# Attention and a routed MoE on one core: rows scattered one tile per iteration, the last three tiles routed each alone

## The chip, the cores and the metric

One core of a Trainium2 chip. The metric is the device time of one execution in microseconds. TensorE is PE here, VectorE DVE, ScalarE ACT, GpSimd POOL, and SyncE SP; SP only issues transfers.

## The reference

Three layers, one after another, in float32. First a linear attention with decay, for 2 batches, 8 heads, 768 steps and 48 columns per head:

```python
for t in range(S):
    cur = einsum('bhd,bhe->bhde', u * k[t], v[t])
    y[t] = einsum('bhd,bhde->bhe', r[t], state + cur)
    state = w * state + einsum('bhd,bhe->bhde', k[t], v[t])
```

Its output, as 1536 tokens of 384 columns, goes through a mixture of 8 experts. Each token goes to the expert with the largest logit `x @ w_gate`; its place within the expert is the number of earlier tokens that chose the same one, and places from the capacity (384) on are dropped. Expert e computes `relu(x @ w1[e]) @ w2[e]`, and the result is multiplied by the token's softmax probability. The third layer is a gated one: `(silu(x @ w_gate) * (x @ w_val)) @ w_out`, with an inner width of 1536.

## The kernel before

The 1536 tokens are 12 tiles of 128. Attention runs as a software pipeline over `it` from -4 to 12, written out by hand (lines 358 to 411): every engine executes its instructions in the order in which this loop issues them. In iteration `it` the loop finishes tile `it` and prepares later ones:

- `outputs(it)`: PE sums the tile's result in `y` (lines 294, 300). `d_major(it)`: ACT copies it to `xT` (line 312; for the last three tiles DVE copies half, line 309).
- `logits(it - 1)`: DVE sums the router's logits (line 450), ACT copies the tile, token by row, to `xu` (line 452; four buffers).
- `state_update(it + 1)`: DVE adds `zt` (line 285), POOL multiplies it to the new state `Z` (line 286).
- `diag_dve(it + 3)`, `diag_act(it + 3)`: DVE reduces `ruk` to `c` (line 243), ACT makes the diagonal of `AT` from it (line 252).
- `diag_pool(it + 4)`: POOL computes `ruk` (lines 236, 237) and `kd` (line 239).
- `inner(it + 2)`: PE's products into `A` (line 259), DVE selects them into `AT` (line 266).
- `decay(it + 3)`: DVE makes `RK` (line 231).
- `token_major(it)`: PE turns `xT` into `xl` (line 443). `state_pe(it + 2)`: PE sums `U` (line 274).
- `prefetch(it - 3)`: SP loads a block `raw` of expert 0's weights (line 574).

Tiles are routed in batches, `BATCHES`. In iteration `it` the batch whose last tile is `it - 1` is routed: `route1` finds each token's expert (6 small DVE instructions and one of ACT, lines 463 to 470), `place_pe` counts earlier tokens on PE (line 486), `route2` computes probability and row (DVE, lines 493 to 514). Then, for every tile of the batch, ACT scales the rows `xu` by the probability (line 518) and POOL scatters them to their rows of `x_disp` in HBM by an indirect DMA (line 519). All scatters write `x_disp`, so each waits for the landing of the one before it, and a load from `x_disp` waits for the scatters before it; a scatter that follows a load waits for that load.

Expert 0 starts without waiting for the last three tiles' scatters. Its first 224 rows come from two sources: `xr0`, loaded from `x_disp` once tiles 0 to 8 are scattered (SP, line 593, issued in iteration 9 behind those scatters) and turned by PE (`first_rows`, line 350), and the last three tiles, each added by a product of `xu` with a one-hot matrix `hot` made in `route2` (line 508; `first_add`, line 342). These sums are copied out of PSUM as `x_plain` (line 608), and the expert's first products follow (line 742). The scaled rows of the last three tiles go to `xs`, since `xu` is still needed.

Expert 1's block `xr` is loaded by SP from `x_disp` behind all scatters (line 593), and PE turns it in the middle of expert 0's second half (line 711). Between the two loads of `xr` SP issues four blocks `raw`; behind the second one it issues expert 1's and later weights. `place_id` scatters token numbers to `ids` on POOL during expert 1 (line 795). After the experts follows the gated layer. `general` (line 1007) is a second path that these inputs do not take.

Of the kernel before, what the change touches and what calls it, by code (L numbers as in the profile page):

```python
# [15 lines left out]
AF = mybir.ActivationFunctionType  # L16
# [9 lines left out]
NT = B * NCH  # L26
# [25 lines left out]

NLAST = 3

BATCHES = [(0, 3), (3, 6), (6, 9), (9, 11), (11, 12)]
NBT = 3
FF_WEIGHTS = {"w_gate": [P, KD, 256], "w_val": [P, KD, 256], "w_out": [P, 2, DM]}

# [5 lines left out]
class Kernel:  # L64
# [44 lines left out]
    def attention(self, st):  # L109
        tc, nc, a = self.tc, self.nc, self.a  # L110
# [45 lines left out]
        def warm(n):  # L156
# [7 lines left out]
            out=tmpm, in_=ones, pattern=[[1, P]], compare_op=ALU.is_gt, fill=0.0, base=0, channel_multiplier=-1  # L164
# [16 lines left out]
        for part in (y[:, 0:3], y[:, 3:], U):  # L181
# [18 lines left out]
            out=neq, in0=sq[:, 0], scalar=1.0, in1=w_dm, op0=ALU.mult, op1=ALU.not_equal, accum_out=nbad  # L200
# [3 lines left out]
        for i in range(7):  # L204
            n = 1 << i
# [15 lines left out]

        RK, AT, cc, ruks = {}, {}, {}, {}
        xTs = self.xTs = {}
        self.xl, self.xu, self.batches = {}, {}, BATCHES
        self.row = cp.tile([P, NT], I32, name="row")

        def decay(i):
# [109 lines left out]
        def first_add(i, first, last):  # L337
            xu, _, hot = self.last[i]
            if first:
                px.extend(self.pa_tile() for _ in range(KD))  # L340
            for k in range(KD):
                nc.tensor.matmul(
                    px[k][:, 0:BLK], lhsT=xu[:, k * P:(k + 1) * P], rhs=hot, start=first, stop=last,
                    skip_group_check=True,
                )

        def first_rows(first):
            for k in range(KD):
                for t in range(2):
                    nc.tensor.matmul(  # L350
                        px[k][:, t * BP:(t + 1) * BP], lhsT=self.xr0[:, t, k * P:(k + 1) * P],
                        rhs=ident[0:BP, 0:BP], start=first, stop=first, skip_group_check=True,
                    )
# [4 lines left out]
        for it in range(-4, NT + 1):  # L358
            batch = ends.get(it - 1)
            if ok(it):  # L360
                outputs(it)
                d_major(it)
            if ok(it - 1):
                self.logits(it - 1)
            if it == NT:
                first_add(NT - 2, False, False)
                first_rows(False)
            if batch:
                self.route1(*batch)
            if has_state(it + 1):  # L370
                state_update(it + 1)
            if it == NT:
                self.route2(*batch)
                first_add(NT - 1, False, True)
            if it < 0 and ok(it + 3):
                decay(it + 3)
                load_T(it + 3 + NB)
            if ok(it + 3):
                diag_dve(it + 3)
                diag_act(it + 3)  # L380
            if ok(it + 4):
                diag_pool(it + 4)
                load_rk(it + 4 + NB)
            if ok(it + 2):
                inner(it + 2)
            if batch and it < NT:
                self.place_pe(*batch)
            if it >= 0 and ok(it + 3):
                decay(it + 3)
                load_T(it + 3 + NB)  # L390
            if batch and it < NT:
                self.route2(*batch)
            if it == -3:
                late_tables()
            if it in (-1, 2, 4):
                load_v({-1: 3, 2: 6, 4: 9}[it])
            if it in (-2, 0):
                first = (it + 2) // 2 * ST
                self.clear_rows(self.x_disp[first:first + BLK])
            if it == NT - 1:  # L400
                first_add(NT - 3, True, False)
            if ok(it):
                self.token_major(it)
            if has_state(it + 2):
                state_pe(it + 2)
            if it == NT - NLAST:
                self.x_load(0, self.xr0)
            if it >= 3:
                self.prefetch(it - 3)
            if it in WARMS:  # L410
                warm(WARMS[it])
# [3 lines left out]
            self.x_part_plain(self.x0, k)  # L415
        self.counts = cp.tile([P, E], F32, name="counts")
        self.count()

    def route_rooms(self):
        tp = self.tp  # L420
# [33 lines left out]
    def route1(self, lo, hi):  # L454

        nc, tp, n = self.nc, self.tp, hi - lo
        b3 = lambda x: x.unsqueeze(2).to_broadcast([P, n, E])
        over_tiles = lambda x: x.unsqueeze(1).to_broadcast([P, n, E])
        small = lambda name: tp.tile([P, NBT, E], F32, name=name, tag=name, bufs=1)[:, 0:n]
        lg, oh = self.lg[:, 0:n], self.oh[:, lo:hi]  # L460
        m = self.m = tp.tile([P, 6, NBT], F32, name="m", tag="m", bufs=2)[:, :, 0:n]
        dif, eqr, ex = small("dif"), small("eqr"), small("ex")
        nc.vector.tensor_reduce(m[:, 0], lg, AX.X, ALU.max)
        nc.vector.tensor_sub(dif, lg, b3(m[:, 0]))
        nc.scalar.activation(ex, dif, AF.Exp)
        nc.vector.scalar_tensor_tensor(
            out=eqr, in0=dif, scalar=0.0, in1=over_tiles(self.rev), op0=ALU.is_ge, op1=ALU.mult
        )
        nc.vector.tensor_reduce(m[:, 1], eqr, AX.X, ALU.max)
        nc.vector.tensor_tensor(oh, eqr, b3(m[:, 1]), ALU.is_equal)  # L470
        self.ex = ex
        if n == 1:
            self.place_pe(lo, hi)

    def place_pe(self, lo, hi):

# [13 lines left out]
    def route2(self, lo, hi):  # L490
        nc, tp, n = self.nc, self.tp, hi - lo
        m, pos = self.m, self.posall[:, lo:hi]
        nc.vector.tensor_reduce(m[:, 2], self.ex, AX.X, ALU.add)
        nc.vector.tensor_scalar(out=m[:, 2], in0=m[:, 2], scalar1=1e-9, scalar2=None, op0=ALU.add)
        nc.vector.reciprocal(m[:, 3], m[:, 2])
        nc.vector.tensor_scalar(
            out=m[:, 1], in0=m[:, 1], scalar1=-float(ST), scalar2=float(E * ST), op0=ALU.mult, op1=ALU.add
        )
        sc = tp.tile([P, NBT, E], F32, name="sc", tag="sc", bufs=1)[:, 0:n]
        nc.vector.tensor_mul(sc, self.pos[:, 0:n], self.oh[:, lo:hi])  # L500
        nc.vector.tensor_reduce(pos, sc, AX.X, ALU.add)
        nc.vector.scalar_tensor_tensor(
            out=m[:, 4], in0=pos, scalar=self.cap_f, in1=m[:, 3], op0=ALU.is_lt, op1=ALU.mult
        )
        nc.vector.tensor_add(m[:, 5], pos, m[:, 1])
        for i in range(lo, hi):
            if i in self.last:
                nc.vector.tensor_scalar(
                    out=self.last[i][2], in0=self.slot, scalar1=m[:, 5, i - lo:i - lo + 1],
                    scalar2=m[:, 4, i - lo:i - lo + 1], op0=ALU.is_equal, op1=ALU.mult,  # L510
                )
        nc.vector.tensor_copy(self.row[:, lo:hi], m[:, 5])
        with nc.allow_low_precision("counts of at most a dozen"):
            nc.vector.tensor_reduce(self.ohs, self.oh[:, 0:hi].rearrange("p n e -> p e n"), AX.X, ALU.add)
        for i in range(lo, hi):
            xu = self.xu.pop(i)
            xs = self.last[i][1] if i in self.last else xu
            nc.scalar.activation(xs, xu, AF.Copy, scale=m[:, 4, i - lo:i - lo + 1])
            nc.gpsimd.indirect_dma_start(
                out=self.x_disp, out_offset=bass.IndirectOffsetOnAxis(ap=self.row[:, i:i + 1], axis=0), in_=xs,  # L520
                in_offset=None,
            )

    def count(self):
        cps = self.ps_1.tile([P, E], F32, name="cps", tag="pos")
# [481 lines left out]
    def general(self):  # L1007

        tc, nc, a = self.tc, self.nc, self.a
        self.last, self.batches = {}, [(i, i + 1) for i in range(NT)]  # L1010
        with ExitStack() as ss:
# [10 lines left out]
                out=tmpm, in_=ones, pattern=[[1, P]], compare_op=ALU.is_gt, fill=0.0, base=0, channel_multiplier=-1  # L1022
# [10 lines left out]
            for i in range(NT):  # L1033
                xT = self.xTs[i] = gp.tile([P, HP, P], F32, name="xT", tag="xT", bufs=2)
                nc.vector.memset(xT, 0.0)
                for j in range(2):
                    for hp in range(HP):
                        h = 2 * hp + j
                        nc.sync.dma_start(
                            out=xT[64 * j:64 * j + D, hp],  # L1040
                            in_=y_seq[i * P:(i + 1) * P, h * D:(h + 1) * D].rearrange("t d -> d t"),
                            allow_slow_non_contiguous=True,
                        )
                self.token_major(i)
                self.logits(i)
                self.route1(i, i + 1)
                self.route2(i, i + 1)
            self.count()
            self.order()
            self.places()  # L1050
# [96 lines left out]
```

## Time and profile before

| | us |
|---|---|
| median of 3 runs | 485.7 |
| lowest, highest | 481.73, 487.23 |
| profiled execution | 487.54 |
| its span | 485.8 |

Over the span PE is busy 92%, DVE 60%, ACT 44%, POOL 36%; the mean granted clock of TensorE is 0.95. A row of a timeline gives the start and the busy time in us, the engine, the line, the operation, the tile written and the tiles read, the count of merged instructions, and in brackets the idle time of that engine just before and what ended it. `POOL x_disp <- DMA x_disp` is POOL waiting for a transfer to land. The start of a scatter on POOL is its issue; its landing is seen in what waits for it. A wait for several things is put down to the one that came last by the records.

### The profile page before, as it was taken

Reading aid. Unit: us, or ns where it says so; the run is one execution under the profiler, and the core shown is the slowest. Engines: PE = TensorE matmul, PEld = TensorE weight load, DVE = VectorE, ACT = ScalarE, POOL = GpSimd, SP = SyncE. Lnnn points to the kernel's source line nnn. Section 1 sums busy time; section 2 is a strip of 40 time slices with the busy share of each in tenths; the row PEclk is TensorE's granted clock in tenths of the full one; section 3 lists DMA queues with packets and bytes.
Section 4 is the critical chain, followed back from the end, with each engine's and each line's share of the span. In section 5 each row is a group of like instructions: output and inputs, shape, how many; then the busy total and the mean of one; then the engine's idle time right before and its main releaser. Section 6 shows DMA issues by size and latency. Waiting matters only on the chain. (4 is left out here: it accounts for less than half of the span.)

```text
span 485.8 us, 8388 instructions
## 1 busy us (share of the span) xinstructions
PE 447.1 (92%) x3203; PEld 430.4 (89%) x3203; DVE 291.6 (60%) x552; ACT 211.9 (44%) x467; POOL 176.9 (36%) x161
## 2 busy tenths in 40 slices
PE   7897796689879999999999999999999999999991
PEld 6686675579769999999999899999999999999991
DVE  5778383538748778888937578897868211111110
ACT  1666363316446576666744555424424222130310
POOL 5974654213021122010004355746446433332231
PEclk9798877969989999999999999999999999999996
DMA  7787270054998899764200324323320000100001
GB/s 269 238 304 248 91 293 34 34 190 110 359 305 285 185 255 299 263 197 163 58 9 1 111 84 130 131 74 122 132 66 1 16 34 0 50 0 34 16 20 38
DMA packets 24802, 63.78 MB, mean 131 GB/s; under 512 B 4784, under 2 KB 10032, under 8 KB 24752
## 3 DMA queue, kind: packets, MB, share of 16 engines
q1 hardware_dynamic: 22112, 57.43, 37.1%
q0 software_dynamic: 1920, 4.73, 2.7%
q10 hardware_dynamic: 720, 1.00, 0.8%
q8 instruction: 27, 0.44, 0.4%
q14 instruction: 23, 0.19, 0.1%
HBM read 55.67 MB, written 7.48 MB: 130 GB/s over the span
## 5 line engine op out<-in xcount | busy, mean ns | idle before, releaser
L952 POOL TENSOR_TENSOR al<-sg,ah 128x384 fp32r<-128x384 f32 x48 | 54.2, 1128 | 122.2 <-ACT ah L951 122.2
L585 DVE TENSOR_TENSOR wlo<-raw,whi 128x768 fp32r<-128x768 f32 x60 | 58.1, 968 | 11.7 <-ACT whi L584 10.9
L719 PE MATMUL py<-hc,whi 128*128 128x448 f32 x192 | 64.2, 375 | 0.0
L951 ACT CAST ah<-sg 128x384 fp32r<-128x384 f32 x48 | 24.7, 514 | 78.0 <-DVE sg L948 78.0
L730 PE MATMUL A<-xc,whi 128*128 128x224 f32 x336 | 56.8, 275 | 0.2 <-DVE hc L750 0.2
L720 PE MATMUL py<-hc,wlo 128*128 128x256 f32 x192 | 54.3, 283 | 0.0
L730 PEld LDWEIGHTS A<-xc,whi 128*128 128x128 f32 x336 | 51.0, 192 | 0.5 <-DVE hc L750 0.4
L584 ACT CAST whi<-raw 128x768 fp32r<-128x768 f32 x60 | 49.9, 838 | 2.5 <-PE py L720 1.4
L965 PE MATMUL po<-w_out_hi,ah 128*128 128x384 f32 x144 | 48.6, 337 | 0.0
L967 PE MATMUL po<-w_out_hi,al 128*128 128x384 f32 x144 | 48.5, 337 | 0.0
L966 PE MATMUL po<-w_out_lo,ah 128*128 128x384 f32 x144 | 48.5, 337 | 0.0
L730 PE MATMUL A<-xc,wlo 128*128 128x224 f32 x168 | 46.2, 275 | 0.0
L719 PEld LDWEIGHTS py<-hc,whi 128*128 128x128 f32 x192 | 36.8, 191 | 2.7
L252 ACT ACTIVATE AT<-ident,c 128x128 f32<-128x128 f32 x96 | 29.4, 391 | 19.9 <-DVE c L243 19.9
L974 DVE TENSOR_TENSOR acc<-acc,po 128x384 f32<-128x384 f32 x36 | 19.3, 546 | 30.9 <-PE po L967 30.9
L720 PEld LDWEIGHTS py<-hc,wlo 128*128 128x128 f32 x192 | 37.1, 193 | 0.0
L948 DVE TENSOR_TENSOR sg<-A,sg 128x384 f32<-128x384 f32 x24 | 13.3, 554 | 37.9 <-PE A L945 30.2
L948 DVE TENSOR_TENSOR sg<-g,sg 128x384 f32<-128x384 f32 x24 | 13.3, 554 | 34.5 <-PE g L945 29.7
L795 POOL DMA_INDIRECT ids<-tok,by_expert x12 | 13.9, 1159 | 54.4 <-DMA ids<-tok,by_expert 50.4
L749 ACT ACTIVATE hc<-A 128x224 fp32r<-128x224 f32 x64 | 23.1, 362 | 23.0 <-PE A L730 19.2
L730 PEld LDWEIGHTS A<-xc,wlo 128*128 128x128 f32 x168 | 32.3, 192 | 0.0
L966 PEld LDWEIGHTS po<-w_out_lo,ah 128*128 128x128 f32 x144 | 27.1, 188 | 0.0
(172 smaller groups left out, 1130.4 us busy)
## 6 DMA issues: line engine op xcount, KB each, us to landing
raw<-in_w SPq DMA_DIRECT2D x62, 384.0 KB, 5.9
rkT<-in_rkT SPq DMA_DIRECT2D x12, 512.0 KB, 5.6
rk<-in_rk SPq DMA_DIRECT2D x12, 384.0 KB, 3.7
raw<-in_w_gate SPq DMA_DIRECT2D x6, 768.0 KB, 4.5
raw<-in_w_val SPq DMA_DIRECT2D x6, 768.0 KB, 4.3
raw<-in_w_out SPq DMA_DIRECT2D x6, 768.0 KB, 4.1
x_disp<-zero SPq DMA_DIRECT2D x8, 336.0 KB, 5.8
xr<-x_disp SPq DMA_DIRECT2D x8, 336.0 KB, 5.9
```

Of the source, the lines that this page charges most:

```text
L252: nc.scalar.activation(AT[i][:, j, hp], ident, AF.Copy, scale=c[:, j, hp:hp + 1])
L584: nc.scalar.copy(h_, raw)
L585: nc.vector.tensor_sub(l_, raw, h_.bitcast(F32))
L719: nc.tensor.matmul(ps[:, 0:2 * BLK], lhsT=wh, rhs=xc, start=first, stop=False, skip_group_check=True)
L720: nc.tensor.matmul(ps[:, 0:256], lhsT=wl, rhs=xc[:, 0:256], start=False, stop=last, skip_group_check=True)
L730: self.nc.tensor.matmul(ph[:, HI], lhsT=w[:, k, fs], rhs=x[1][:, k, half], start=(k == 0 and i == 0), stop=(k == KD - 1 and i == 2),)
L948: nc.vector.tensor_mul(sg, pg["w_val"], sg)
L951: nc.scalar.copy(h_, sg)
L952: nc.gpsimd.tensor_sub(l_, sg, h_.bitcast(F32))
L965: nc.tensor.matmul(po, lhsT=ah[:, ts_], rhs=wh, start=(i == 0), stop=False)
L966: nc.tensor.matmul(po, lhsT=ah[:, ts_], rhs=wl, start=False, stop=False)
L967: nc.tensor.matmul(po, lhsT=al[:, ts_], rhs=wh, start=False, stop=(i == len(parts) - 1))
```

## The change

The scatters leave `route2`: it only appends its tiles to a list `to_scatter`, and a new function `scatter`, called once per iteration (twice in iteration 10) behind `route2`, scales and scatters the oldest tile of the list. What is left when the loop ends is scattered behind the copies to `x_plain` and the final count. Tiles 9 and 10 are now routed each alone, so there is one batch more. Tile 9's one-hot products (`first_add(NT - 3, ...)`) move ahead of `place_pe` in iteration 11. In iteration 12 `place_pe` stands between tile 10's one-hot products and `first_rows`. The first load of `xr` moves from iteration 9 to iteration 10. The path `general` calls the new function too.

```diff
-BATCHES = [(0, 3), (3, 6), (6, 9), (9, 11), (11, 12)]
+BATCHES = [(0, 3), (3, 6), (6, 9), (9, 10), (10, 11), (11, 12)]
...
             if ok(it - 1):
                 self.logits(it - 1)
+            if batch:
+                self.route1(*batch)
             if it == NT:
                 first_add(NT - 2, False, False)
+                self.place_pe(*batch)
                 first_rows(False)
-            if batch:
-                self.route1(*batch)
...
+            if it == NT - 1:
+                first_add(NT - 3, True, False)
             if batch and it < NT:
                 self.place_pe(*batch)
...
             if batch and it < NT:
                 self.route2(*batch)
+            for _ in range(2 if it == NT - 2 else 1):
+                if self.to_scatter and it < NT:
+                    self.scatter()
...
-            if it == NT - 1:
-                first_add(NT - 3, True, False)
...
-            if it == NT - NLAST:
+            if it == NT - 2:
                 self.x_load(0, self.xr0)
...
         self.count()
+        while self.to_scatter:
+            self.scatter()
...
         self.ex = ex
-        if n == 1:
-            self.place_pe(lo, hi)
...
-        for i in range(lo, hi):
-            xu = self.xu.pop(i)
-            xs = self.last[i][1] if i in self.last else xu
-            nc.scalar.activation(xs, xu, AF.Copy, scale=m[:, 4, i - lo:i - lo + 1])
-            nc.gpsimd.indirect_dma_start(
-                out=self.x_disp, out_offset=bass.IndirectOffsetOnAxis(ap=self.row[:, i:i + 1], axis=0), in_=xs,
-                in_offset=None,
-            )
+        self.to_scatter += [(i, m[:, 4, i - lo:i - lo + 1]) for i in range(lo, hi)]
+
+    def scatter(self):
+
+        i, scale = self.to_scatter.pop(0)
+        xu = self.xu.pop(i)
+        xs = self.last[i][1] if i in self.last else xu
+        self.nc.scalar.activation(xs, xu, AF.Copy, scale=scale)
+        self.nc.gpsimd.indirect_dma_start(
+            out=self.x_disp, out_offset=bass.IndirectOffsetOnAxis(ap=self.row[:, i:i + 1], axis=0), in_=xs,
+            in_offset=None,
+        )
```

POOL's order at the first batch, iterations 3 to 5. The numbers behind a name tell its buffers apart: `xu_423`, `xu_490` and `xu_559` are tiles 0, 1 and 2. Before:

```order
L239 TENSOR_TENSOR kd1_126<-rk1_88,wk_tok_187 128x384
L519 DMA x_disp_65<-xu_423,row_194 14080x384
L519 DMA x_disp_65<-xu_490,row_194 14080x384
L519 DMA x_disp_65<-xu_559,row_194 14080x384
L236 TENSOR_TENSOR ruk_666<-rk2_89 128x384
```

and now:

```order
L239 TENSOR_TENSOR kd1_126<-rk1_88,wk_tok_187 128x384
L527 DMA x_disp_65<-xu_423,row_194 14080x384
L236 TENSOR_TENSOR ruk_662<-rk2_89 128x384
L237 TENSOR_TENSOR ruk_662<-ruk_662,u_b_93 128x384
L239 TENSOR_TENSOR kd2_127<-rk2_89,wk_tok_187 128x384
L527 DMA x_disp_65<-xu_490,row_194 14080x384
L236 TENSOR_TENSOR ruk_733<-rk0_87 128x384
```

One scatter now stands between the work of two iterations where three stood in a row.

PE's order from tile 11's token rows to the last one-hot products, where `xr` are the rows loaded from `x_disp` and `hot10`, `hot11` the one-hot matrices of tiles 10 and 11. Before:

```order
L443 MATMUL xl_1165<-IW_196,xT_1123 128x104 x4
L342 MATMUL A_1159<-hot10_208,xu10_206 128x224
L350 MATMUL A_1159<-ident_104,xr_212 128x112 x2
L486 MATMUL pos_1196<-oh_200,before_195 128x8
L342 MATMUL A_1159<-hot11_211,xu11_209 128x224
```

and now:

```order
L449 MATMUL xl_1187<-IW_196,xT_1148 128x104 x4
L342 MATMUL A_1164<-hot10_208,xu10_206 128x224
L490 MATMUL pos_1212<-oh_200,before_195 128x8
L350 MATMUL A_1164<-ident_104,xr_212 128x112 x2
L342 MATMUL A_1164<-hot11_211,xu11_209 128x224
```

The counting product `pos` of tile 11 has moved ahead of the rows from `xr`.

SP's order from the last attention input (`rkT`) to expert 1's block. Before:

```order
L124 DMA rkT_86<-in_rkT 128x1024
L574 DMA raw<-in_w 128x768 x4
L593 DMA xr<-x_disp 112x2x384
L574 DMA raw<-in_w 128x768 x4
L593 DMA xr<-x_disp 112x2x384
```

and now:

```order
L124 DMA rkT_86<-in_rkT 128x1024
L582 DMA raw<-in_w 128x768 x5
L601 DMA xr<-x_disp 112x2x384
L582 DMA raw<-in_w 128x768 x3
L601 DMA xr<-x_disp 112x2x384
```

One weight block has moved ahead of the first load from `x_disp`.

## Rows read from the trace of the kernel before

**Rows 1.** Timeline of POOL, batches one and two: start us, us, engine, line, work [idle before].

```profile
44.63 1.16 POOL L519 DMA_INDIRECT x_disp<-xu,row  x1 [1.77 <-ACT xu L518]
50.19 0.96 POOL L519 DMA_INDIRECT x_disp<-xu,row  x1 [4.40 <-DMA x_disp<-xu,row]
53.56 0.96 POOL L519 DMA_INDIRECT x_disp<-xu,row  x1 [2.41 <-ACT xu L452]
54.54 1.00 POOL L236 TENSOR_TENSOR ruk<-rk 128x384 f32<-128x384 f32 x1
...
68.41 1.01 POOL L519 DMA_INDIRECT x_disp<-xu,row  x1 [1.63 <-ACT xu L518]
73.82 0.96 POOL L519 DMA_INDIRECT x_disp<-xu,row  x1 [4.40 <-DMA x_disp<-xu,row]
...
78.13 0.60 POOL L286 TENSOR_TENSOR Z<-zt,Wm 112x192 f32<-112x192 f32 x1
```

**Rows 2.** Timeline of DVE, ACT and PE around the two stalls.

```profile
43.53 1.63 ACT L518 ACTIVATE xu<-xu,m 128x384 f32<-128x384 f32 x3 [2.36 <-DVE m L505]
...
51.70 1.16 PE L259 MATMUL A<-RK 48*128 48x128 f32 x16
...
56.65 0.55 DVE L243 TENSOR_REDUCE c<-ruk 128x8 f32<-128x384 f32 x1 [5.84 <-POOL ruk L237]
57.12 1.34 DVE L266 COPY_PREDICATED AT<-mask,A 128x512 f32<-128x512 uint8 x2
...
78.76 0.36 DVE L285 TENSOR_TENSOR zt<-U,Z 112x192 f32<-112x192 f32 x1 [6.54 <-POOL Z L286]
```

**Rows 3.** Timeline of POOL, third batch and the last three tiles.

```profile
89.20 1.01 POOL L519 DMA_INDIRECT x_disp<-xu,row  x1 [2.67 <-ACT xu L518]
93.83 0.96 POOL L519 DMA_INDIRECT x_disp<-xu,row  x1 [3.62 <-DMA x_disp<-xu,row]
97.16 0.96 POOL L519 DMA_INDIRECT x_disp<-xu,row  x1 [2.37 <-ACT xs L518]
103.81 0.96 POOL L519 DMA_INDIRECT x_disp<-xs,row  x1 [5.69 <-DMA xr<-x_disp]
109.73 0.96 POOL L519 DMA_INDIRECT x_disp<-xs,row  x1 [4.96 <-ACT x_plain L608]
114.96 0.96 POOL L519 DMA_INDIRECT x_disp<-xs,row  x1 [4.27 <-DVE hc L750]
```

**Rows 4.** Timeline of SP's queue, the transfers it issues.

```profile
60.01 1.96 SPq L574 DMA_DIRECT2D raw<-in_w  x4
99.74 0.33 SPq L593 DMA_DIRECT2D xr<-x_disp  x1
100.11 1.88 SPq L574 DMA_DIRECT2D raw<-in_w  x4
118.25 0.33 SPq L593 DMA_DIRECT2D xr<-x_disp  x1
```

**Rows 5.** Timeline of PE, the end of attention and expert 1's turn.

```profile
103.06 1.59 PE L350 MATMUL A<-ident,xr 112*128 112x112 f32 x12 [0.42 <-DMA xr<-x_disp]
...
106.00 2.58 PE L342 MATMUL A<-hot,xu 128*128 128x224 f32 x6 [1.31 <-DVE row L512]
...
124.38 0.79 PE L711 MATMUL px<-ident,xr 112*128 112x112 f32 x6 [2.43 <-DMA xr<-x_disp]
```

**Rows 6.** Windows: us, busy (instructions) of each engine, granted PEclk, DMA share, GB/s.

```profile
core 0: us, PE busy (x) PEld busy (x) DVE busy (x) ACT busy (x) POOL busy (x), PEclk, DMA share, GB/s
73.00:89.00 16.00, 12.05 (x138) 10.02 (x132) 7.73 (x26) 5.04 (x15) 5.60 (x7) 0.79 0.07 26
89.20:97.20 8.00, 4.50 (x46) 3.69 (x47) 3.60 (x21) 3.63 (x10) 2.01 (x3) 0.89 0.15 51
121.90:145.00 23.10, 17.50 (x130) 16.83 (x130) 14.60 (x26) 9.84 (x23) 3.39 (x3) 0.96 1.02 337
```

**Rows 7.** Timeline of POOL in the last of these windows.

```profile
126.60 0.96 POOL L795 DMA_INDIRECT ids<-tok,by_expert  x1 [6.58 <-DMA ids<-tok,by_expert]
```

More of the change, by code (lines that the diff above doesn't have):

```diff
@@ L223, in attention @@
         xTs = self.xTs = {}
-        self.xl, self.xu, self.batches = {}, {}, BATCHES
+        self.xl, self.xu, self.batches, self.to_scatter = {}, {}, BATCHES, []
         self.row = cp.tile([P, NT], I32, name="row")
@@ L1046, in general @@
                 self.route1(i, i + 1)
+                self.place_pe(i, i + 1)
                 self.route2(i, i + 1)
+                self.scatter()
             self.count()
```

## The prediction

> **What bounds the kernel now.** I read the windows by stage first, then the timeline of POOL, since it is the engine the diff rearranges, then the engines that wait for POOL, and last SP's queue and the hand-over from attention to the experts. The reader should see four things.
>
> First, POOL stands still around its scatters. Batch one's three scatters start at 44.63, 50.19 and 53.56 us, and the next piece of attention work, `ruk`, only at 54.54 [rows 1]. Each scatter waits until the one before it has landed: start to start that is 5.56 and 3.37 us, in the second batch 5.41 for its first pair, in the third 4.63 and 3.33 [rows 1, 3].
>
> Second, DVE pays for it twice. It idles 5.84 us before `c` at 56.65, which needs that `ruk`, and 6.54 us before `zt` at 78.76, which needs the `Z` that POOL starts at 78.13, behind batch two's scatters [rows 2, 1]. The third batch blocks nothing on DVE, as POOL has no attention work left behind it.
>
> Third, from the third batch on there is a chain that no arithmetic shortens: scatters 6, 7, 8 at 89.20, 93.83, 97.16, the load of `xr` on SP at 99.74, scatters 9, 10, 11 at 103.81, 109.73, 114.96, then SP's next load of `xr` at 118.25, for expert 1 [rows 3, 4]. PE waits 2.43 us for that last load before its transposes at 124.38 [rows 5]. So the end of the chain, and not PE's arithmetic, sets when expert 1 starts.
>
> Fourth, the DMA engines are nearly empty before that chain (share 0.07, 26 GB/s, in 73 to 89) and full behind it (share 1.02, 337 GB/s, in 121.9 to 145) [rows 6]. The transfers behind it are issued by SP, which stands in the chain itself. If the chain moves, they move with it.
>
> **The change part by part.** Times are those of the profiled execution: 487.54 us, of which the span is 485.8 and 1.74 lies outside it. The median of the runs shown is 485.7, which is 1.84 below the profiled time; I carry that difference through at the end. A change within 1%, about 4.9 us, is about what a measurement of this kernel cannot tell from none.
>
> *One scatter per iteration, first batch.* POOL goes on to `ruk` after one scatter, at 44.63 + 1.16 = 45.8 instead of 54.54 [rows 1]. That is 8.7 us earlier, more than the 5.84 that DVE idles, so this idle goes whole. What is late next is PE: the select into `AT` at 57.12 needs inner products that PE starts at 51.70 and ends at 52.86 [rows 2]. These come earlier too, as ACT no longer does three scalings (1.63 us) ahead of the next `xT` but one: 2 x 0.54 = 1.1 us. The select can start at 52.9 - 1.1 = 51.8. Gain: 57.1 - 51.8 = **5.3 us**.
>
> *Second batch.* `Z` now stands behind one scatter. The 6.54 us before `zt` go. The two scalings saved on ACT would give another 1.1 us, but I leave that as cover for `ruk`, which shares POOL with a scatter in each iteration now. Gain: **6.5 us**. By DVE alone scatter 6 would start at 89.20 - 5.3 - 6.5 = 77.4.
>
> *The scatters as a pace of their own.* Each still waits for the one before, and behind a waiting scatter POOL holds the next `Z` and `ruk`, for which DVE waits. Six hops lie between scatter 0 at 44.63 and scatter 6. The trace shows hops from 3.33 to 5.56 us. With all six at the upper one, scatter 6 starts at 44.63 + 33.4 = 78.0; with all at 4.63, at 72.4, and then DVE decides. What the trace does not show is a scatter in the middle of the loads' burst, which moves closer: the four `raw` loads that SP issues at 60.01 [rows 4] will now be released while scatters run. The nearest row for a full DMA is the `ids` scatter at 126.60, one hop of 0.96 + 6.58 = 7.54 us [rows 7]. So a hop costs 3.3 to 7.5 us; I take 5.6, the nearest in kind, and add a little for two hops in the burst: scatter 6 at 78.2, so 0.8 us of the gain is lost (bounds: none, and 12.5 at six hops of 7.54).
>
> The Trainium skill has a rule that speaks against putting scatters beside DVE work ("SBUF — State Buffer", "SBUF: two separate sides"): a transfer issued by POOL has its descriptors written by POOL's cores, and while DVE holds the port that the two share, they cannot be written, so the transfer starts late. The trace leaves room for it: the slow hops, 5.56 and 5.41, are those at whose start DVE was at work, and the quick ones, 3.37 and 3.33, had little DVE work beside them. But those slow hops also had loads beside them. If the rule holds, all six hops are slow, and the sum would be the 78.0 above; without it, 77.4. The rival below takes its worse reading.
>
> *One more batch for routing.* Tiles 9 and 10 are routed apart. That adds about 16 small DVE instructions; in 89.2 to 97.2 DVE spends 3.60 us on 21 of them [rows 6], so 2.7 us, one `ex` on ACT and a pair of tiny products on PE. They fall between scatter 6 and scatter 8, where the chain only waits for landings (8.0 us, DVE busy 3.6). Cost: nothing; if DVE were late there, up to 2.7.
>
> *The tail on PE.* The products for tile 11's place move ahead of the rows from `xr`, so the 1.31 us before PE's last one-hot products at 106.00 go, and tile 9's one-hot products no longer wait inside iteration 11 [rows 5]. The expert's first products start about 1.3 us earlier against the chain. That is worth nothing: PE then waits 2.43 + 1.3 us for expert 1's `xr`. The last two scatters are scaled behind the copies out of PSUM, but scatter 10 waits for scatter 9's landing in any case.
>
> *SP's queue.* The load of `xr` moves one iteration later but keeps its place behind scatter 8, and one `raw` load passes it. So three loads instead of four follow it [rows 4] and run beside scatter 9. A load of 0.39 MB at 337 GB/s is 1.17 us; the slow hop behind scatter 9 (5.92) may lose all of it or none. I take **0.5 us**.
>
> Sum: -5.3 - 6.5 + 0.8 + 0 - 0.5 = **-11.5 us**. Profiled, 487.54 - 11.5 = 476.0; less 1.84, **474.2 us**.
>
> **The rivals.**
>
> *Scatters set the pace and cost more than the waits they replace.* Between scatters 0 and 6 the kernel before takes 44.57 us, or 7.43 per tile; so from a mean hop of 7.43 us on the change is slower. The `ids` hop of 7.54 shows that a full DMA reaches this. At 8.5 us the six hops take 51.0, 6.4 more than now, and all of attention follows, as `Z` and `ruk` are queued behind the scatters: 492.1 us. Against it: the four `raw` loads at 60.01 are 1.6 MB, 4.7 us at 337 GB/s; with the loads just ahead of them perhaps twice that, so two hops in six can meet the burst. Chance 0.05.
>
> *Half the gain.* Hops of 6.5 us, because DVE and POOL disturb each other throughout (the skill's rule at its worse reading): scatter 6 at 44.63 + 39 = 83.6, a gain of 5.6 + 0.5, so 479.6 us. The `xu` buffers pull the same way: there are four, each is now read for longer, and ACT has to wait for a scatter's landing before it overwrites one. Chance 0.13.
>
> *Hidden anyway.* The stretch after 121.9 is full of weight loads; if those were paced by something that does not move, attention would just end earlier and PE wait: 485.7. Against it: nothing is in flight in 73 to 89, and SP issues the loads only after the chain. Chance 0.07.
>
> *More.* If the ACT scalings also count in the second batch (1.1) and scatter 9 gains the whole 1.17, the sum is -13.3: 472.4. Chance 0.12.
>
> **How the numbers follow.** The forecast, 474.2 with some 2 us either way, has 0.63. Below 480.8 (1% faster) lie it, the last rival, and two thirds of the half gain: 0.84. Within 1% the hidden case and the rest of the half gain: 0.11. Slower by over 1%: 0.05. The range runs from 469.5 (the larger gain and a low draw of runs: those shown differ by 5.5 us) to 480.5, which takes in the half gain and leaves out the two rivals above it.
>
> **What would show it.** Right: between scatters 0 and 6 POOL does attention work between any two scatters, scatter 6 starts near 78, the DVE idles before `c` and `zt` are under 2 us, expert 0's first products start 12 to 13 us earlier, PE's wait for expert 1's `xr` grows to 3 to 4 us, and everything behind is shifted by about 11.5. The first term fails if `c` still waits for `ruk`; the third if hops of over 6 us follow one another; the last if the stretch behind the chain grows by what attention lost. The forecast is wrong if the time is above 481.

## The result, and the profile after

| | before | after |
|---|---|---|
| median, us | 485.2 (4 runs) | 471.55 (4 runs) |
| lowest, highest | 481.73, 487.23 | 468.19, 473.12 |
| ratio | | 0.9717, 95% interval 0.9637 to 0.9797 |
| profiled execution, its span | 487.54, 485.8 | 468.19, 466.4 |

The changed kernel is faster. It was measured twice more, beside the experiments: ratios 0.9778 (0.9735 to 0.9821) and 0.9805 (0.9761 to 0.985). Weighted by their intervals the three make 0.978, give or take 0.003: 10.6 us of 482. The predicted 474.2 against 485.7 is 0.976. The profiled execution of before took longer than any of its four runs, and that of after is the shortest of its own, so their distance, 19.4 us, overstates the change; stages are compared below by distances within a trace.

POOL in the changed kernel, the scatters of tiles 0 to 6 (start us, us, engine, line, work, and in brackets the idle time before):

```profile
44.17 1.16 POOL L527 DMA_INDIRECT x_disp<-xu,row  x1 [2.04 <-ACT xT L312]
...
49.44 1.02 POOL L527 DMA_INDIRECT x_disp<-xu,row  x1
...
55.26 1.01 POOL L527 DMA_INDIRECT x_disp<-xu,row  x1 [0.75 <-ACT xu L458]
...
63.63 1.01 POOL L527 DMA_INDIRECT x_disp<-xu,row  x1 [2.87 <-DVE AT L266]
...
67.56 1.01 POOL L527 DMA_INDIRECT x_disp<-xu,row  x1 [0.15 <-issue]
...
71.88 1.01 POOL L527 DMA_INDIRECT x_disp<-xu,row  x1 [2.68 <-ACT xu L526]
...
77.72 1.01 POOL L527 DMA_INDIRECT x_disp<-xu,row  x1 [2.63 <-ACT xu L526]
```

Between any two of the first six scatters stands attention work (the lines left out: `ruk`, `kd`, `Z`), and scatter 6 starts 33.55 us after scatter 0. Before it was 44.57 [rows 1, 3]. DVE, where it waited for POOL:

```profile
48.36 0.55 DVE L243 TENSOR_REDUCE c<-ruk 128x8 f32<-128x384 f32 x1 [0.48 <-POOL ruk L237]
...
50.63 1.35 DVE L266 COPY_PREDICATED AT<-mask,A 128x512 f32<-128x512 uint8 x2 [1.71 <-PE A L259]
...
65.40 0.36 DVE L285 TENSOR_TENSOR zt<-U,Z 112x192 f32<-112x192 f32 x1 [0.39 <-POOL Z L286]
...
67.44 0.56 DVE L243 TENSOR_REDUCE c<-ruk 128x8 f32<-128x384 f32 x1 [1.68 <-POOL ruk L237]
```

The waits of 5.84 before `c` and 6.54 before `zt` [rows 2] are 0.48 and 0.39 now; one of 1.68 before a later `c` is left, and the select at 50.63 waits for PE, as the prediction had it ("what is late next is PE"). The chain behind scatter 6, POOL and then SP's queue:

```profile
84.44 0.96 POOL L527 DMA_INDIRECT x_disp<-xu,row  x1 [2.37 <-DMA x_disp<-xu,row]
91.24 0.96 POOL L527 DMA_INDIRECT x_disp<-xs,row  x1 [5.84 <-DVE ohs L518]
96.83 0.96 POOL L527 DMA_INDIRECT x_disp<-xs,row  x1 [4.63 <-DVE offs_i L831]
100.26 0.96 POOL L527 DMA_INDIRECT x_disp<-xs,row  x1 [2.47 <-DVE wlo L593]
```

```profile
54.06 2.34 SPq L582 DMA_DIRECT2D raw<-in_w  x5
87.02 0.33 SPq L601 DMA_DIRECT2D xr<-x_disp  x1
87.39 1.41 SPq L582 DMA_DIRECT2D raw<-in_w  x3
103.73 0.33 SPq L601 DMA_DIRECT2D xr<-x_disp  x1
```

From scatter 8 to SP's load of expert 1's block it is 19.3 us, where it was 21.1 [rows 3, 4]. SP now issues five weight blocks at 54.06, beside scatter 2, and three behind the load of `xr`. PE at four places:

```profile
44.21 1.14 PE L449 MATMUL xl<-IW,xT 128*128 128x104 f32 x8 [1.62 <-ACT xT L312]
...
62.51 1.49 PE L449 MATMUL xl<-IW,xT 128*128 128x104 f32 x8 [2.25 <-ACT xT L312]
...
90.49 2.90 PE L350 MATMUL A<-ident,xr 112*128 112x112 f32 x12 [1.03 <-DMA xr<-x_disp]
...
109.40 0.74 PE L719 MATMUL px<-ident,xr 112*128 112x112 f32 x6
```

The first two are waits for ACT. The first stands where the kernel before had a longer one, since ACT now does one scaling ahead of `xT` instead of three:

```profile
45.68 2.03 PE L443 MATMUL xl<-IW,xT 128*128 128x104 f32 x8 [3.05 <-ACT xT L312]
```

The second is new. The last row is the start of expert 1's transposes: no wait stands there, where it was 2.43 us [rows 5]. In the other two traces of this kernel there is one; the second one's row:

```profile
113.06 0.79 PE L719 MATMUL px<-ident,xr 112*128 112x112 f32 x6 [2.94 <-DMA xr<-x_disp]
```

### The profile page after: what moved, and what is told of

Its sections match the earlier page's. It is cut to its first block, busy times and chain, and to the rows that moved or that the text cites. A ratio compares the mean times of both kernels' runs of the same rounds, so it can differ in the third digit from the quotient of the medians.

```text
span 466.4 us, 8409 instructions
## 1 busy us (share of the span) xinstructions
PE 439.6 (94%) x3204; PEld 424.0 (91%) x3204; DVE 293.2 (63%) x567; ACT 211.5 (45%) x468; POOL 179.0 (38%) x161
## 5 line engine op out<-in xcount | busy, mean ns | idle before, releaser
L727 PE MATMUL py<-hc,whi 128*128 128x448 f32 x192 | 63.1, 370 | 0.0
L959 ACT CAST ah<-sg 128x384 fp32r<-128x384 f32 x48 | 24.7, 515 | 78.2 <-DVE sg L956 78.2
L982 DVE TENSOR_TENSOR acc<-acc,po 128x384 f32<-128x384 f32 x36 | 19.3, 546 | 30.9 <-PE po L975 30.9
L955 ACT ACTIVATE sg<-A 128x384 f32<-128x384 f32 x24 | 11.7, 486 | 34.7 <-PE A L953 34.7
```

The costliest lines, as they stand in the source:

```text
L727: nc.tensor.matmul(ps[:, 0:2 * BLK], lhsT=wh, rhs=xc, start=first, stop=False, skip_group_check=True)
L959: nc.scalar.copy(h_, sg)
```

## The experiments

Twelve runs were made, in three groups of four, each group on one chip: ten edits, and the changed kernel twice. A group shares its runs of the kernel before (medians 482.14, 482.28, 481.84 us). The table has each one's ratio to the kernel before, and from its one trace the us from scatter 0 to scatter 6, from scatter 6 to scatter 11, and PE's summed wait for the blocks of experts 1 and 2.

| kernel | ratio, 95% interval | 0 to 6 | 6 to 11 | PE's wait |
|---|---|---|---|---|
| before | 1 | 44.57 | 25.76 | 5.60 |
| changed, first | 0.9717 (0.9637 to 0.9797) | 33.55 | 22.54 | 0 |
| changed, second | 0.9778 (0.9735 to 0.9821) | 33.58 | 23.30 | 2.94 |
| changed, third | 0.9805 (0.9761 to 0.9850) | 37.29 | 23.66 | 1.71 |
| 1 spread alone | 0.9828 (0.9790 to 0.9865) | 32.91 | 24.15 | 3.81 |
| 2 no spread | 0.9973 (0.9942 to 1.0004) | 44.46 | 23.36 | 2.73 |
| 3 first batch together | 0.9871 (0.9829 to 0.9913) | 37.58 | 24.28 | 2.09 |
| 4 second batch together | 0.9915 (0.9885 to 0.9944) | 38.31 | 23.17 | 2.82 |
| 5 four loads behind | 0.9756 (0.9716 to 0.9796) | 35.76 | 23.43 | 0.90 |
| 6 pair routed | 0.9776 (0.9730 to 0.9821) | 35.54 | 22.71 | 3.69 |
| 7 scatter an iteration later | 0.9791 (0.9750 to 0.9832) | 29.72 | 24.80 | 2.90 |
| 8 loads from ACT | 0.9824 (0.9782 to 0.9867) | 36.36 | 23.09 | 3.07 |
| 9 scale after copy | 0.9836 (0.9802 to 0.9870) | 40.08 | 26.15 | 2.56 |
| 10 both | 0.9879 (0.9833 to 0.9925) | 35.84 | 25.75 | 1.90 |

TensorE's clock is not the same in these stretches either. From scatter 0 to scatter 6, in the kernel before, without the spread (experiment 2), and in the changed kernel's three traces, in this order:

```profile
core 0: us, PE busy (x) PEld busy (x) DVE busy (x) ACT busy (x) POOL busy (x), PEclk, DMA share, GB/s
44.60:89.20 44.60, 35.01 (x408) 29.90 (x408) 24.72 (x63) 20.73 (x61) 20.87 (x21) 0.77 0.38 145
44.70:89.20 44.50, 34.90 (x408) 29.69 (x408) 24.72 (x64) 20.75 (x61) 20.90 (x22) 0.77 0.41 153
44.20:77.70 33.50, 30.07 (x408) 25.51 (x408) 26.23 (x63) 20.25 (x59) 22.21 (x21) 0.90 0.56 201
46.30:79.90 33.60, 28.60 (x408) 24.47 (x408) 29.19 (x63) 20.41 (x60) 22.83 (x21) 0.95 0.53 201
44.80:82.10 37.30, 32.84 (x408) 27.94 (x408) 28.95 (x64) 20.18 (x59) 22.94 (x22) 0.82 0.50 182
```

The granted clock (PEclk) is 0.77 where the scatters stand together and 0.82 to 0.95 where they are spread, and the same 408 matmuls keep PE busy for 35 us or for 29 to 33. The edits show what the spread brings as a whole; how much of it is the waits that go, and how much the clock that comes with it, no run here tells apart.

**The changed kernel again**, twice, without an edit.

> The changed kernel itself, beside the other three on one chip, so that they can be compared with it. The first measurement gave a ratio of 0.972 to the kernel before; the same is expected within 0.006. In its trace expert 1's transposes start without a wait, or with under 1 us.

> The changed kernel again, beside the next three on one chip. Expected: a ratio of 0.972 to 0.978 to the kernel before, and 33.6 us from scatter 0 to scatter 6, as in its two traces so far.

The ratios came out at 0.9778, as expected, and 0.9805, just above the range. In the second trace expert 1's transposes waited 2.94 us, where no wait or under 1 us was expected. The third trace took 37.29 us from scatter 0 to scatter 6, not 33.6: the same program differs by some 4 us there from one execution to another, which is the yardstick for single traces below.

**1. The spread alone**, an edit of the kernel before (the new function `scatter` and the path `general` as in the change):

```diff
...
-        for i in range(lo, hi):
...
+        self.to_scatter += [(i, m[:, 4, i - lo:i - lo + 1]) for i in range(lo, hi)]
+        while self.to_scatter and self.to_scatter[0][0] >= 6:
+            self.scatter()
...
                 self.route2(*batch)
+            if self.to_scatter:
+                self.scatter()
```

> The kernel before with one part of the change alone: the scatters of the first two batches (tiles 0 to 5) go one per iteration; the third batch, the last three tiles, the order on PE and the load of xr stay as before. Theory (POOL's wait behind the scatters is the gain): scatter 6 starts near 78 us instead of 89.20, the waits of DVE before c and zt fall under 2 us each, and the time falls by 10 to 12 us. Rival (the last three tiles' routing and SP's order carry a good part): the time falls by less than 8 us, although scatter 6 starts near 78.

Scatter 6 started at 77.72, as the theory had it. In 36 to 92 us DVE waits for POOL only once and not before `zt` at all (us in total, times, longest us):

```profile
DVE c L243 <- POOL ruk L237: 0.5, 1, 0.5
```

The time fell by 1.72%, 8.3 us (6.5 to 10.1): below the theory's 10 to 12, and at the rival's edge of 8. The spread of six tiles is most of the change; the rest is 2.3 of the 10.6 us, give or take 2.3.

**2. No spread**, an edit of the changed kernel:

```diff
-            for _ in range(2 if it == NT - 2 else 1):
-                if self.to_scatter and it < NT:
-                    self.scatter()
+            while self.to_scatter and self.to_scatter[0][0] < NT - NLAST:
+                self.scatter()
+            if it == NT - 1:
+                self.scatter()
```

> The changed kernel with the scatters of the first three batches issued together again, each batch's three at its routing; tiles 9 and 10 stay routed alone, and PE's order and the later load of xr stay too. Theory: POOL blocks as before, DVE idles 5 to 7 us before c and zt, scatter 6 starts near 89, and only 0 to 3 us of the change remain against the kernel before. Rival: 4 us or more remain, from the end of attention.

DVE's waits in 36 to 92 us (us in total, times, longest us):

```profile
DVE c L243 <- POOL ruk L237: 9.1, 2, 7.5
DVE zt L285 <- POOL Z L286: 6.2, 1, 6.2
```

Both stalls are back, scatter 6 starts at 89.16, and 1.3 us of the change are left (3 to none), the theory's 0 to 3. From the other side this shows the same as the first experiment: taking the spread out of the changed kernel costs 9.3 us, give or take 2.0.

**3 and 4. One batch together**, with `3 if it == 3` or `3 if it == 6`:

```diff
-            for _ in range(2 if it == NT - 2 else 1):
+            for _ in range(3 if it == 3 else 2 if it == NT - 2 else 1):
```

> The changed kernel with the first batch's three scatters issued together in iteration 3; all else stays. Theory, first term of the sum: 5.3 us slower than the changed kernel, and scatter 6 starts near 83 instead of 77.72, with some 5 us of DVE's idle before c back. Rival (a later wait takes the place, as the second batch's spread absorbs it): under 3 us slower.

> The changed kernel with the second batch's three scatters issued together in iteration 6; all else stays. Theory, second term of the sum: 6.5 us slower than the changed kernel, with DVE's idle before zt of 5 to 7 us back, and scatter 6 near 84. Rival (the two stalls overlap in what they hold up): under 4 us slower.

DVE's waits with the first batch together, then with the second:

```profile
DVE c L243 <- POOL ruk L237: 6.2, 2, 5.7
```

```profile
DVE zt L285 <- POOL Z L286: 5.4, 1, 5.4
```

Each stall comes back alone, at its place. Scatter 6 does not show it: 37.58 and 38.31 us after scatter 0, where the changed kernel's third trace has 37.29. Against the changed kernel's 0.978, which is from the other groups, the first costs 0.009, 4.4 us, give or take 2.5 (5.3 were predicted), and the second 0.0135, 6.5 us, give or take 2.0 (6.5 were predicted). The rivals' bounds of 3 and 4 us are passed by the middle values, in the first case not by the whole interval.

**5. Four loads behind `xr`:**

```diff
-            if it >= 3:
+            if it >= 3 and it != NT - 3:
                 self.prefetch(it - 3)
...
             if it == NT - 2:
                 self.x_load(0, self.xr0)
+                self.prefetch(it - 4)
```

> The changed kernel with the sixth weight block (unit 6) loaded behind the first load of xr again, so that four loads instead of three follow it; all else stays. Prediction's term: 0.5 us slower than the changed kernel, 1.2 at most. Rival (this load is what made scatters 9 to 11 slow and PE wait for the blocks of experts 1 and 2): the hop from scatter 9 to 11 grows from 9.0 to 11 us, PE waits 2 us or more for expert 1's block, and the time grows by 2 to 4 us.

No effect: 0.9756 beside 0.9778, which is 1.1 us faster, give or take 2.8; scatter 9 to 11 took 10.3 us beside 9.8 in the same group, and PE's wait was 0.90. The rival falls; the prediction's 0.5 us is too small to be told from nothing.

**6. Tiles 9 and 10 routed as a pair:**

```diff
-BATCHES = [(0, 3), (3, 6), (6, 9), (9, 10), (10, 11), (11, 12)]
+BATCHES = [(0, 3), (3, 6), (6, 9), (9, 11), (11, 12)]
...
-            if it == NT - 1:
-                first_add(NT - 3, True, False)
             if batch and it < NT:
                 self.place_pe(*batch)
...
+            if it == NT - 1:
+                first_add(NT - 3, True, False)
             if ok(it):
                 self.token_major(it)
```

> The changed kernel with tiles 9 and 10 routed as a pair again, tile 9's one-hot products behind that routing as before; the spread scatters, the moved load of xr and the moved counting product stay. Theory: the chain from scatter 6 to scatter 8 only waits for landings, so the time stays within 1 us of the changed kernel; PE reaches expert 0 up to 1.5 us later. Rival (PE, not the chain, now sets the end): 1.5 to 3 us slower.

0.9776 beside 0.9778: no difference, give or take 3.0 us, as the theory had it. Routing the two tiles alone neither costs nor brings time that these runs can tell; they do not exclude the rival's 1.5 to 3 us.

**7. Scatters one iteration later:**

```diff
+            if it < NT - NLAST:
+                for _ in range(2 if it == NT - NLAST - 1 else 1):
+                    if self.to_scatter:
+                        self.scatter()
             if batch and it < NT:
                 self.route2(*batch)
-            for _ in range(2 if it == NT - 2 else 1):
-                if self.to_scatter and it < NT:
-                    self.scatter()
+            if it >= NT - NLAST:
+                for _ in range(2 if it == NT - 2 else 1):
+                    if self.to_scatter and it < NT:
+                        self.scatter()
...
-        xu = self.xu[i] = self.last[i][0] if i in self.last else tp.tile([P, DM], F32, name="xu", tag="xu", bufs=4)
+        xu = self.xu[i] = self.last[i][0] if i in self.last else tp.tile([P, DM], F32, name="xu", tag="xu", bufs=6)
```

> The changed kernel with the scatters of the first two batches issued ahead of the routing in their iteration instead of behind it, so that ACT never holds the next tile's copy back for a scale that is not there yet; tiles 0 to 3 go one iteration later, tiles 4 and 5 both in iteration 8; six xu buffers instead of four. Theory: PE's waits of 1.62 and 2.25 us before xl in iterations 4 and 7 go, and the time falls by 2 to 4 us below the changed kernel. Rival (scatters 4 and 5 together in iteration 8 hold Z and scatter 6 back again): scatter 6 starts no earlier than 77.7, and the time does not fall, or grows by up to 3 us.

POOL, scatters 0 and 6:

```profile
51.55 1.16 POOL L532 DMA_INDIRECT x_disp<-xu,row  x1 [3.94 <-ACT xu L531]
...
81.27 1.01 POOL L532 DMA_INDIRECT x_disp<-xu,row  x1 [1.77 <-ACT ex L476]
```

The rival holds. PE's waits before `xl` are gone, but scatter 0 starts 5.2 us later than in the changed kernel's trace of the same group (46.34), and the quicker hops do not win that back: scatter 6 comes at 81.27 beside 79.92. The ratio, 0.9791, does not differ from the changed kernel's.

**8. Weight blocks from ACT's queue:**

```diff
         if k < 8:
-            self.unit_load(0, k)
+            self.unit_load(0, k, self.nc.scalar if k < 7 else None)
```

> The changed kernel with weight blocks 0 to 6 issued from ACT's queue, where each keeps to its own iteration, instead of from SP, which issues five of them in one go at 54 us; the bytes and DVE's work stay. It tells apart what made scatter 2 land only after 7.6 us. Theory (the loads' burst): it lands in under 5 us, scatter 3 starts 1 to 2 us sooner after scatter 0, and the time falls by 0 to 2 us. Rival (DVE's work keeps POOL from writing descriptors, which is unchanged here): it still takes over 6.5 us to land.

Inconclusive for its question. Scatter 1, issued at 53.27, held back ACT's next copy into its buffer until 61.90:

```profile
61.90 0.48 ACT L458 COPY xu<-xl 128x384 f32<-128x384 f32 x1 [5.54 <-DMA x_disp<-xu,row]
```

That is over 8 us, but loads were still running: attention's own, with one weight block, issued at 51.45 to 53.67, made 272 GB/s in 53.3 to 62.5. The time, 0.9824 beside 0.9805 in the same group, tells nothing either. The third trace of the changed kernel has the better test, in three windows that begin with scatters 1, 2 and 3 (us, busy time and instructions of each engine, granted PEclk, DMA share, GB/s):

```profile
core 0: us, PE busy (x) PEld busy (x) DVE busy (x) ACT busy (x) POOL busy (x), PEclk, DMA share, GB/s
51.00:58.20 7.20, 7.20 (x104) 6.10 (x100) 5.40 (x13) 5.09 (x15) 4.99 (x5) 0.97 0.97 354
58.20:66.00 7.80, 4.43 (x69) 3.68 (x67) 7.63 (x16) 3.96 (x12) 5.36 (x5) 0.94 0.78 285
66.00:70.70 4.70, 4.70 (x45) 4.03 (x46) 4.18 (x6) 2.66 (x9) 4.42 (x4) 0.50 0.11 42
```

and the scatter that ends the last of them:

```profile
70.72 1.01 POOL L527 DMA_INDIRECT x_disp<-xu,row  x1 [0.16 <-issue]
```

With the DMA engines at a share of 0.97 and 0.78 the next scatter came 7.15 and 7.86 us later. With a share of 0.11 it came after 4.69 us, of which POOL waited 0.16 for a landing or anything else, while DVE was busy 4.18 of 4.70 us. The loads go with slow landings; DVE's work alone did not make one here. Not all of the second hop is landing: it holds the routing of tiles 3 to 5, and ACT began to scale tile 3 only at 64.27. The Trainium skill's rule ("SBUF — State Buffer", "SBUF: two separate sides") is about DVE operations that hold the port shared with POOL; read as in the prediction, for any work of DVE, it would have made the third hop slow. This window does not bear that reading out.

**9. The scale behind the next iteration's copies:**

```diff
             if ok(it - 1):
                 self.logits(it - 1)
+            if it <= NT - NLAST and self.to_scatter:
+                self.scatter()
...
-            for _ in range(2 if it == NT - 2 else 1):
+            for _ in range(2 if it == NT - 2 else 1 if it >= NT - NLAST else 0):
```

> The changed kernel with ACT's scaling of tiles 0 to 5 moved behind the next iteration's two copies; POOL's order stays word for word. In the changed kernel ACT waits 2.67 and 2.96 us for the scale while the next tile's sums lie ready, and PE waits 1.62 and 2.25 us for the copy. Theory: these waits of PE go, scatter 0 starts where it did, and the time falls by 1.5 to 3 us below the changed kernel. Rival (DVE, busy throughout in those iterations, sets the pace): under 1 us.

0.9836 beside 0.9805 in the same group: no gain. Neither side named what the trace shows, which is that of the slowest of its six runs (479.57 us; the others took 472.92 to 476.72). ACT now waits for landings, since the four `xu` buffers are read by scatters for longer than it takes to come round to them:

```profile
49.56 0.48 ACT L460 COPY xu<-xl 128x384 f32<-128x384 f32 x1 [2.63 <-DMA x_disp<-xu,row]
...
58.55 0.48 ACT L460 COPY xu<-xl 128x384 f32<-128x384 f32 x1 [5.20 <-DMA x_disp<-xu,row]
```

In the changed kernel the same wait is there, but shorter: 1.37 and 0.71 us in its second and third trace, and in the first

```profile
62.93 0.48 ACT L458 COPY xu<-xl 128x384 f32<-128x384 f32 x1 [0.47 <-DMA x_disp<-xu,row]
```

The slowest hop of this trace has another cause. From scatter 4 at 71.16 to scatter 5 it took 9.41 us, with the DMA engines almost empty:

```profile
80.57 1.01 POOL L529 DMA_INDIRECT x_disp<-xu,row  x1 [7.77 <-DVE zt L285]
```

```profile
core 0: us, PE busy (x) PEld busy (x) DVE busy (x) ACT busy (x) POOL busy (x), PEclk, DMA share, GB/s
71.20:80.60 9.40, 9.40 (x86) 7.99 (x82) 4.26 (x12) 3.81 (x12) 1.60 (x3) 0.52 0.06 21
```

PE was busy throughout, at a granted clock of 0.52, the lower of its two levels (1.2 GHz) for nearly all of it; in 59.8 to 71.2 it had been busy 6.6 of 11.4 us at 1.00 and then 0.88. DVE (`xT`) and through it ACT waited for its products.

**10. Both edits, 8 and 9:**

> The two edits before together. If both causes are right, they add up: 2 to 4 us below the changed kernel, with under 31.5 us from scatter 0 to scatter 6. Rival (the last scatters and expert 1's block set the end whatever attention does): scatter 6 comes earlier, but PE's wait for expert 1's block takes what was gained.

0.9879, no better than either, with 35.84 us from scatter 0 to 6; beside 0.9805 in the same group it is 3.6 us slower, give or take 3.1, and the cause stays open. Neither expectation was met, as neither edit had brought scatter 6 forward. No version ran faster than the changed kernel beyond the intervals.

## Why the prediction was right, and where it was wrong

*First batch, 5.3 us.* Right: `c` waits 0.48 us, the select waits for PE instead, and experiment 3 puts the price of the stall at 4.4, give or take 2.5.

*Second batch, 6.5 us.* Right: experiment 4 measures 6.5, give or take 2.0, and the wait before `zt` returns with it.

*The scatters' own pace, 0.8 us lost.* Right in size in two of three traces: 33.55 and 33.58 us to scatter 6, where the prediction has 78.2 - 44.63 = 33.6; in the third it is 37.29. That the size fits is in part luck. The prediction has all six hops near 5.6 and set by landings; in the first trace they run from 3.93 to 8.37. The first three scatters land in 4.4, 5.0 and 7.6 us beside the loads, the next three in 2.6, and their hops of 3.93, 4.32 and 5.84 are longer than the 3.33 that a landing of 2.6 allows [rows 1]: there attention and the routing set the pace, not the scatters. The rival of dear hops named the right mechanism for the first three; the mean hop stays at 5.6 to 6.2 us, and the break-even of 7.43 is not reached. The `xu` buffers, named under the half gain, became a real limit, as experiment 9 shows.

*One more batch, nothing.* Right (experiment 6).

*SP's queue, 0.5 us.* Not shown: experiment 5 cannot tell it from nothing.

*Hidden anyway.* This rival fell: the time went down with scatter 6, and from scatter 11 to the end of the span the three traces take 366.1, 368.1 and 367.9 us, where it was 370.8. The stretch behind the chain did not grow by what attention lost.

*The tail on PE, nothing; PE's wait for expert 1's block grows to 3 to 4 us.* Expert 0's first products come 12.5 and 13.2 us sooner after scatter 0 in the first two traces, where 12 to 13 were expected, and 9.0 in the third. The wait is the step that failed. It was 0, 2.94 and 0.92 us, and the wait for experts 1 and 2 together 0 to 2.94 instead of 5.60. The prediction let the chain behind scatter 6 move as it was, but for 0.5; it became shorter, 22.5 to 23.7 us from scatter 6 to 11 instead of 25.76. Experiment 2, with the scatters together, has 23.36 there, and the spread alone 24.15. So it is shorter with the other parts of the change as well as with the spread. It does not follow from the order alone, though: experiment 9, whose order behind scatter 6 is the changed kernel's, has 26.15 in its one, slow trace. The other parts' 1.3 us (experiment 2) to 2.3 us (10.6 less 8.3) were counted as 0.5; neither is clear of 0.5, or of nothing. Which of them it is stays open: the moved load and the routing showed no effect one by one (5, 6), within some 3 us, and the counting product ahead of `xr`'s rows and the late scaling of the last two tiles were not tried alone. With one trace of the kernel before, which took longer than its runs, part of the 25.76 may be that execution's own.

*The sum.* The spread was put at 11.0 and measures 8.3 alone (6.5 to 10.1) and 9.3 by its removal (7.3 to 11.3); the rest was put at 0.5 and measures 1.3 to 2.3, with intervals that begin at nothing. By the middle values the two errors go against each other, so 11.5 stands beside a measured 10.6 (13.65 in the first four runs). TensorE's clock is in no term, although it was 0.77 between scatters 0 and 6 before and 0.82 to 0.95 after.

## What to carry to other kernels

Indirect transfers into one tensor ran one after another here, and the engine that issued three in a row stood until the third could be issued: put other work of that engine between them, and look for the engine that idles behind it. That idle is about what there is to gain: 12.4 us of DVE here, of which the spread brought 8.3 to 9.3. Before the issue is spread, count how many buffers the transfers hold at their slowest landing, beside the loads that will then run with them. Once the stall was gone, four further edits (7 to 10), each aimed at a wait that was left, brought nothing.

## What the runs showed of the hardware

A scatter of 128 rows of 1536 bytes landed after 2.6 us at best and 7.6 at worst in the same execution (the profile's row for the line, changed kernel):

```profile
DMA to landing us min/median/max: 2.6/2.6/7.6
```

The slow one is scatter 2, issued at 55.26 with the DMA engines at a share of 1.01 and 365 GB/s until 62.9. Scatter by scatter, in the same trace:

| scatter | 0 | 1 | 2 | 3 | 4 | 5 |
|---|---|---|---|---|---|---|
| landed after, us | 4.4 | 5.0 | 7.6 | 2.6 | 2.6 | 2.6 |
| next scatter after, us | 5.27 | 5.82 | 8.37 | 3.93 | 4.32 | 5.84 |
| DMA share until then | 0.67 | 0.85 | 0.98 | 0.20 | 0.14 | 0.10 |

The other two traces agree: 4.2, 5.1 and 6.6 us, and 5.5, 6.4 and 7.1, for the first three scatters, and 2.6 to 2.9 for those of the next three whose landing is on record. So a scatter beside loads landed up to three times later than one with the DMA engines nearly empty, and a weight block that nobody waits for yet may hold back a transfer that is waited for. Which of the loads it is, the weights' or attention's own, experiment 8 did not tell apart.
